# Gated attention and a token-mixing MLP on one core: the order of loads, casts and first pairs in the opening

## The chip, the core and the metric

The kernel runs on one core of one Trainium2 chip. The core has a matrix engine (TensorE, PE in the profile), a vector engine (VectorE, DVE), a scalar engine (ScalarE, ACT), a general engine (GpSimd, POOL) and SyncE (SP), which here only issues DMAs. ACT and POOL issue DMAs too; a DMA that changes the type (v and z from fp32 to fp16) is issued by POOL here. The metric is the device time of one execution in microseconds (us); less is better. Three runs of the kernel before gave a median of 792.01 us.

## The reference

```python
# u, v: (8, 3200, 256), z: (8, 3200, 64)
scores = (1.0 / S) * np.matmul(z, z.transpose(0, 2, 1))
attn = np.maximum(scores, 0.0) ** 2
x = u * np.matmul(attn, v)
# w_q, w_k: (256, 64), w_out: (256, 256)
wq = x @ w_q
wk = x @ w_k
W_tok = (1 / 8) * np.einsum('bsd,btd->bst', wq, wk)
mixed = np.einsum('bst,btd->bsd', W_tok, x)
return np.maximum(mixed, 0.0) @ w_out
```

There is no softmax, so the scores of a batch are a symmetric matrix, and squared ReLU keeps it so.

## The kernel before

**Tiles and groups.** A batch has 3200 rows, which is 25 tiles of 128. The output rows are worked on in seven groups, six of 512 rows and one of 128. For a group, each of the 25 row tiles gives a block of scores, 128 by 512. Scores are made two blocks at a time, called a pair (`use_pair`, L585): two matmuls on the two halves of the array (`scores`, L223) into one of two PSUM buffers (`sc`). The first stage (`first_stage`) takes the pair out of PSUM with ReLU, on ACT (L242) or DVE (L246), into `g`. The second stage (`second_stage`) squares it into fp16, on ACT (L259) or POOL (L261), into one of 14 buffers `at`. The second product (`second_product`, L302) multiplies these blocks with v, into four PSUM banks `acc`. A row tile of a group costs 8 second products, two for each of four 128-column parts.

**Symmetry.** A block of a near group isn't computed twice: SyncE turns it with a transposing DMA (`tt`, `ttl`, L281) and the later group uses the turned block. So a buffer of `at` comes free only when its turned copy has been taken and its second products have run.

**A group's end.** When the second products of half a group are complete, ACT copies one bank out (`both`, L318), DVE adds the other (L319), and POOL multiplies with u (L323) into `x_sb`. SyncE turns x (L348); projections with `wqk` (L365), the products of keys and x (L402), and, a batch later, the mixing (L430) and the output projection with `wo` (L453) follow.

**The order is written by a planner in the kernel.** All engines run their instructions in the order in which the Python code emits them. A loop at the end keeps an estimated clock for each of PE, DVE, ACT and POOL, for SyncE's queue (`sp_at`) and for the DMA engines (`dma_at`), and chooses what to emit next: a pair, a step of second products, or other work. `at_time(t, fn)` emits something when the planner's clock of PE has reached t; `move(ready, due, issue, takes, fn, landed, may)` puts a DMA of SyncE in line, to be emitted after `ready`, in order of `due`. None of these times exists on the chip: there, an instruction waits for its operands and for what stands ahead of it in its engine's queue.

**The opening.** `load_first_z` loads z of batch 0 in four chunks (tiles 0 to 3, 12 to 17, 18 to 24, 4 to 11), one of them from ACT's queue, into buffers with the tag `x_sb`. `load_first_v` loads v from POOL's queue, first tiles 0 and 1, then 2 and 3, and later 12 to 17, 18 to 24 and 4 to 11. `cast_first` (L119) makes two fp16 copies of each z chunk, on DVE, ACT and POOL; `turn_first` turns them on TensorE with an identity (L125) and copies the result into `zT` (L132). Then come the first two pairs. `load_u` (L163) loads u for a group from SyncE's queue into one of two buffers `u_sb`. `load_weights` (L183) loads `wo`, the four parts of `wqk` and the two of `wk2`; the `wo` buffer has the tag `x_sb`. `cast_weights` (L188, L189) casts them on POOL at planner time 38. `batch_begun` plans the next batch's z (load, two copies on DVE, five turned pieces, L155) and its v (five loads from POOL's queue, L138). `open_rows` chooses the row tiles whose second products come next; in the first group of batch 0 it also asks for the planned arrival `v_at` of v. `cold` makes matmuls dearer in the planner's first 11 us.

Of the kernel before, what the change touches and what calls it, by code (L numbers as in the profile page):

```python
# [16 lines left out]
def kernel(  # L17
# [36 lines left out]
    NEARBY = 8  # L54

# [116 lines left out]
    wo32 = {}  # L172

    def load_weights():
        wo32[0] = px.tile([P, ND, D], FP32, tag="x_sb", name="wo32")
        loads = [(wo32[0][:], moe_w_out.rearrange("(c p) e -> p c e", p=P))]
        for r in range(2):
            for w32, w in ((wq32, moe_w_q), (wk32, moe_w_k)):
                loads.append((w32[top(r), :, :], w.rearrange("(c p) h -> p c h", p=dh)))
        for half in range(2):  # L180
            loads.append((wk2[:, :, half, :], moe_w_k.rearrange("(c p) h -> p c h", p=P)))
        for i, (t, w) in enumerate(loads):
            move(18.0 + i, 26.0 + i, 0.65, 0.5, lambda t=t, w=w: nc.sync.dma_start(out=t, in_=w))  # L183

    def cast_weights():
        for r in range(2):
            for w32, half in ((wq32, r), (wk32, 1 - r)):
                nc.gpsimd.tensor_copy(out=wqk[top(r), :, half, :], in_=w32[top(r), :, :])  # L188
        nc.gpsimd.tensor_copy(out=wo[:], in_=wo32[0][:])  # L189
# [334 lines left out]
    keys_at, out_of, turned_at, z_at = {}, {}, {}, {}  # L524
# [49 lines left out]
    def cold():  # L574
        return 2.0 if clock[PE] < 11.0 else 1.0
# [131 lines left out]

    def batch_begun(b, t):
        if b + 1 < B:
            t += 6 if b == 0 else 0  # L710
            at_time(t + 6, lambda: (load_z(b + 1), push(3.0)))
            for half in range(2):
                at_time(
                    t + 18 + 3 * half,
                    lambda half=half: (double_z(b + 1, half), give(DVE, clock[PE], 0.98)),
                )
# [41 lines left out]
    def open_rows():  # L758
# [8 lines left out]
        if b == 0 and gi == 0:  # L767
            ready = [t for t in ready if v_at[t] <= clock[PE]]
# [4 lines left out]
        if len(take) < want:  # L773
            if closing and len(left) - len(take) < 4:
                take = take[: len(left) - 4]
            if not take or (fresh and len(take) < (6 if b or gi else 2)):
                return False
            if not closing:
                take = take[: max(0, len(left) - 4)]
# [61 lines left out]
    load_first_v(0, 2)  # L841
    cast_first(0)
    cast_first(1)
    load_first_v(2, 2)
# [5 lines left out]
    clock[:] = [4.5, 4.95, 4.7, 7.8]  # L850
    v_at = [4.5] * 2 + [8.2] * 2 + [18.7] * 8 + [11.2] * 6 + [14.7] * 7
# [13 lines left out]
    at_time(38.0, cast_weights)  # L865
# [6 lines left out]
    while groups or work or current["left"]:  # L872
# [16 lines left out]
        able = p < NPAIR and z_at[p_chunk(p)] <= now and (p < NAT or all_used(p - NAT) and turned_at.get(p - NAT, 0.0) <= now and not out_of.get(p - NAT))  # L889
# [131 lines left out]
```

## Time and profile before

| | |
|---|---|
| runs | 788.74, 792.01, 792.71 us; median 792.01 |
| the profiled execution | 790.19 us |
| its span, first to last instruction | 787.4 us |
| mean granted clock of TensorE | 0.995 |
| busy, share of the span | PE 97%, DVE 61%, ACT 71%, POOL 80% |
| DMA over the span | 141.52 MB, mean 180 GB/s |

The page gives busy times by engine, the span in 40 slices, the DMA queues, the chain of work that ended last, the costliest groups of instructions by line, and the DMA issues. Other views of the same trace give the instructions in order of time (a timeline, with neighbours of one kind merged), the busy time of each engine in chosen windows, and who waited for whom. PE busy counts a matmul from its start to its modelled end; matmuls overlap, so the count of matmuls in a window says more than its busy time. "SPq" is SyncE's queue: how long the issue of a DMA held it. The granted clock is the share of full speed at which TensorE's clock was let through.

### The profile page before, as it was taken

The numbers are of one execution on the slowest core, as the hardware profiler recorded it, in microseconds if no ns is written. First come the engines' busy times: TensorE is split into PE (matmuls) and PEld (weight loads), VectorE is DVE, ScalarE is ACT, GpSimd is POOL, SyncE is SP. The second block draws the span as 40 slices with busy tenths as digits, with TensorE's granted clock in tenths as the row PEclk, the third lists the DMA queues.
The fourth block names the chain that finished last, engine by engine and source line by source line (L and its number), as shares of the span: only waits on it lengthen the run. The fifth ranks groups of instructions, "written<-read, shape, count | busy, mean of one in ns | idle before, by whom it ended". The sixth has DMA issues, their size and how long they took to land.

```text
span 787.4 us, 28277 instructions
## 1 busy us (share of the span) xinstructions
PE 766.3 (97%) x12373; PEld 659.4 (84%) x12373; DVE 480.9 (61%) x494; ACT 562.9 (71%) x668; POOL 631.0 (80%) x524
## 2 busy tenths in 40 slices
PE   6989999999999999999999999999999999999985
PEld 5879989888898878988899788987889888898883
DVE  5654768566676576755466567656557555675522
ACT  6766677766787757886678667787687876777725
POOL 8878597897889798988689987978789977688640
PEclk9999999999999999999999999999999999999998
DMA  7999999998999999999999998999989999779335
GB/s 196 149 165 165 173 191 162 204 233 167 160 172 224 186 195 178 165 207 187 198 161 182 196 215 176 175 149 222 222 172 155 204 198 198 150 145 199 113 82 196
DMA packets 310075, 141.52 MB, mean 180 GB/s; under 512 B 287808, under 2 KB 290752, under 8 KB 309952
## 3 DMA queue, kind: packets, MB, share of 16 engines
q1 hardware_dynamic: 303040, 123.55, 83.3%
q0 software_dynamic: 6768, 15.98, 13.8%
q8 instruction: 96, 1.57, 0.9%
q14 instruction: 27, 0.22, 0.1%
q10 hardware_dynamic: 144, 0.20, 0.1%
HBM read 59.64 MB, written 26.21 MB: 109 GB/s over the span
## 4 chain that ended last, share of the span: by engine, by line
PE 88%; POOL 3%; DMA 2%; issue 2%; ACT 1%; DVE 1%; SPq 1%; DVEq 0%; POOLq 0%; ACTq 0%
PE acc L302 64%; PE sc L223 12%; PE fo L453 6%; PE qk L365 3%; PE qk L402 2%; POOL at L261 2%; PE mx L430 1%; DVE g L246 1%; DMA v_sb<-in_v_dram 1%; SPq L281 1%; DMA out_dram<-fo 1%; DMA kx<-qk 1%; POOL x_sb L323 0%; DMA z<-in_z_dram 0%; ACT g L242 0%
## 5 line engine op out<-in xcount | busy, mean ns | idle before, releaser
L261 POOL TENSOR_TENSOR at<-g 128x1024 f16<-128x1024 f32 (+2 forms) x240 | 441.1, 1851 | 68.2 <-DVE g L246 58.0
L302 PE MATMUL acc<-v_sb,at 64*128 64x256 f16 x7312 | 492.5, 269 | 2.8 <-DMA v_sb<-in_v_dram 1.9
L246 DVE TENSOR_SCALAR g<-sc 128x1024 f32<-128x1024 f32 (+1 forms) x303 | 357.9, 1197 | 155.7 <-PE sc L223 148.3
L302 PEld LDWEIGHTS <-at 64*128 64x128 f16 x7312 | 394.4, 94 | 60.6 <-issue 7.9
L259 ACT ACTIVATE at<-g 128x1024 f16<-128x1024 f32 (+1 forms) x228 | 234.5, 1035 | 18.9 <-DVE g L246 16.2
L242 ACT ACTIVATE g<-sc 128x1024 f32<-128x1024 f32 (+2 forms) x165 | 165.0, 1002 | 50.6 <-PE sc L223 48.3
L223 PE MATMUL sc<-zT 64*128 64x512 f16 x920 | 178.2, 378 | 2.6 <-DVE g L246 2.1
L323 POOL TENSOR_TENSOR x_sb<-both,u_sb 128x512 f16<-128x512 f32 (+1 forms) x112 | 132.8, 1192 | 50.9 <-DVE both L319 50.6
L302 PE MATMUL acc<-v_sb,tt 64*128 64x256 f16 x2304 | 161.2, 269 | 0.0
L302 PEld LDWEIGHTS <-tt 64*128 64x128 f16 x2304 | 126.7, 94 | 13.0
L319 DVE TENSOR_TENSOR both<-acc,both 128x512 f32<-128x512 f32 (+1 forms) x104 | 69.7, 670 | 86.9 <-ACT both L318 80.8
L318 ACT COPY both<-acc 128x512 f32<-128x512 f32 (+1 forms) x104 | 58.8, 566 | 75.8 <-PE acc L302 73.2
L478 ACT ACTIVATE fo<-fo 128x1024 f32<-128x1024 f32 (+2 forms) x54 | 48.0, 889 | 26.3 <-PE fo L453 23.8
L223 PEld LDWEIGHTS <-zT 64*128 64x128 f16 x920 | 56.5, 94 | 12.2 <-issue 7.9
L443 ACT ACTIVATE rt<-mx 128x1024 f16<-128x1024 f32 (+1 forms) x56 | 52.1, 934 | 8.6 <-PE mx L430 8.0
L453 PE MATMUL fo<-wo,rt 128*128 128x256 f16 x400 | 52.8, 274 | 1.8 <-ACT rt L443 1.8
L378 ACT CAST qk<-qk 128x512 f16<-128x512 f32 (+1 forms) x54 | 29.3, 543 | 34.7 <-PE qk L402 27.3
L453 PEld LDWEIGHTS <-rt 128*128 128x128 f16 x400 | 35.0, 98 | 15.9 <-issue 10.0
L417 DVE TENSOR_TENSOR ha<-qk,ha 128x512 f32<-128x512 f32 x37 | 25.6, 691 | 26.9 <-ACT qk L378 26.0
L365 PE MATMUL qk<-xT_sb,wqk 64*128 64x256 f16 (+1 forms) x404 | 32.0, 265 | 0.5 <-DMA xT_sb<-x_sb 0.5
L395 POOL COPY kx<-kx 128x128 f16<-128x128 f16 (+1 forms) x101 | 26.1, 285 | 7.3 <-DMA kx<-qk 7.3
L402 PE MATMUL qk<-x_sb,kx 64*128 64x256 f16 x360 | 29.0, 269 | 0.0
(43 smaller groups left out, 218.4 us busy)
## 6 DMA issues: line engine op xcount, KB each, us to landing
u_sb<-in_u_dram SPq DMA_DIRECT2D x48, 512.0 KB, 4.7
out_dram<-fo SPq DMA_DIRECT2D x40, 512.0 KB, 5.2
v_sb<-in_v_dram POOLq DMA_DIRECT2D x35, 320.0 KB, 6.1
out_dram<-fo SPq DMA_DIRECT2D x16, 256.0 KB, 2.0
zn<-in_z_dram POOLq DMA_DIRECT2D x7, 400.0 KB, 6.1
tt<-at SPq DMA_TRANSPOSE x144, 4.5
u_sb<-in_u_dram SPq DMA_DIRECT2D x8, 128.0 KB, 3.7
out_dram<-fo SPq DMA_DIRECT2D x8, 128.0 KB, 1.9
```

The costliest lines, as they stand in the source:

```text
L223: nc.tensor.matmul(out=sc[:, h, 0:gw], lhsT=zT[b][top(h), ts(ti, P)], rhs=zT[b][top(h), ds(gs, gw)], start=True, stop=True,)
L242: nc.scalar.activation(out=g[:, hs, 0:w], in_=sc[:, hs, 0:w], func=RELU, scale=GSCALE)
L246: nc.vector.tensor_scalar(out=g[:, hs, 0:w], in0=sc[:, hs, 0:w], scalar1=0.0, scalar2=GSCALE, op0=AOP.max, op1=AOP.mult,)
L259: nc.scalar.square(out=out, in_=g[:, hs, 0:w])
L261: nc.gpsimd.tensor_mul(out=out, in0=g[:, hs, 0:w], in1=g[:, hs, 0:w])
L302: nc.tensor.matmul(out=accs[half, r][:, ds((j % 2) * D, D)], lhsT=weights(b, gi, ti, j)[top(r), :], rhs=vs[b][top(r), ti, :], start=(first ...
L318: nc.scalar.copy(out=both[:, 0 : n * D], in_=accs[half, 0][:, 0 : n * D])
L319: nc.vector.tensor_add(out=both[:, 0 : n * D], in0=accs[half, 1][:, 0 : n * D], in1=both[:, 0 : n * D])
L323: nc.gpsimd.tensor_mul(out=xs[b, gi][:, 0:n, :, r, :].rearrange("p n c d -> p (n c) d"), in0=both[:, 0 : n * D].rearrange("p (m d) -> p m ...
L365: nc.tensor.matmul(out=ps[:, r, 0 : n * P], lhsT=wqk[top(r), c, :, :].rearrange("p t h -> p (t h)"), rhs=xTs[b, gi][top(r), 0:n, c, :], st ...
L443: nc.scalar.activation(out=out, in_=ps[:, 0:nr, 0 : ND * n * P], func=RELU)
L453: nc.tensor.matmul(out=banks[r][:, ds(j * D, D)], lhsT=flat[:, ds((dc * n + j) * P, P)], rhs=wo[:, dc, :], start=(dc == 0 and j == 0), sto ...
```

## The change

- **v of batch 0.** Tiles 0 to 3 come in one load instead of two; the other three loads keep their order on POOL's queue.
- **z and u of batch 0.** The third and fourth chunk of z are loaded into buffers with the tag `u_sb`, so that the first two loads of u reuse them.
- **TensorE.** 28 matmuls of the identity with itself stand ahead of everything else.
- **First pairs.** `first_stage` can split a pair's two blocks between ACT and DVE. `use_pair` does so up to planner time 24 where by its clocks the two halves end sooner than the whole. In the emitted order DVE has eight more instructions of its kind, 128 by 512.
- **Weights.** `wo` gets a buffer with the tag `fo`, is loaded at 76 to 80 and cast on POOL at 90. The two halves of `wk2` are loaded at 110 to 130. The cast of `wqk` is at 40 instead of 38.
- **z and v of batch 1.** z is loaded at 24, as before, and its five turned pieces are planned 4 us apart instead of 6. Its five v loads are planned 8 us apart from 64 instead of 13 us apart from 38. For later batches these times stay.
- **The planner's knowledge.** `v_at` now holds the planned arrival of v for every batch, and the first group of each batch asks for it. `z_here` holds back the pairs of a batch until the last turned piece of its z has landed by the planner's clock. `cold` is 1.4 for 9 us instead of 2.0 for 11, and the planned arrivals of the first v are other numbers. `KEEP` names the number 4.

```diff
     def load_first_z():
         for i, (n0, nn) in enumerate(ZCH):
-            z32[n0] = px.tile([P, nn, dqk], FP32, tag="x_sb", name="z32")
+            pool, tag = (px, "x_sb") if i < 2 else (pu, "u_sb")
+            z32[n0] = pool.tile([P, nn, dqk], FP32, tag=tag, name="z32")
...
     def load_weights():
-        wo32[0] = px.tile([P, ND, D], FP32, tag="x_sb", name="wo32")
-        loads = [(wo32[0][:], moe_w_out.rearrange("(c p) e -> p c e", p=P))]
+        loads = []
         for r in range(2):
             for w32, w in ((wq32, moe_w_q), (wk32, moe_w_k)):
                 loads.append((w32[top(r), :, :], w.rearrange("(c p) h -> p c h", p=dh)))
+        for i, (t, w) in enumerate(loads):
+            move(18.0 + i, 26.0 + i, 0.65, 0.4, lambda t=t, w=w: nc.sync.dma_start(out=t, in_=w))
         for half in range(2):
-            loads.append((wk2[:, :, half, :], moe_w_k.rearrange("(c p) h -> p c h", p=P)))
-        for i, (t, w) in enumerate(loads):
-            move(18.0 + i, 26.0 + i, 0.65, 0.5, lambda t=t, w=w: nc.sync.dma_start(out=t, in_=w))
+            t, w = wk2[:, :, half, :], moe_w_k.rearrange("(c p) h -> p c h", p=P)
+            move(110.0, 130.0, 0.65, 0.4, lambda t=t, w=w: nc.sync.dma_start(out=t, in_=w))
+        wo32 = pg.tile([P, 2, W], FP32, tag="fo", name="wo32", bufs=2)[:, 0, :]
+        wo32 = wo32.rearrange("p (c e) -> p c e", c=ND)
+        w = moe_w_out.rearrange("(c p) e -> p c e", p=P)
+        move(76.0, 80.0, 0.65, 0.8, lambda: nc.sync.dma_start(out=wo32, in_=w))
+        at_time(40.0, cast_weights)
+        at_time(90.0, lambda: (nc.gpsimd.tensor_copy(out=wo[:], in_=wo32), give(POOL, 0.0, 0.6)))
...
-    def first_stage(p, sc, on_act):
+    def first_stage(p, sc, ways):
         g = pg.tile([P, 2, W], FP32, tag="g", name="g")
-        for hs, w in pieces(p):
+        parts = pieces(p)
+        if len(ways) > len(parts):
+            parts = [(slice(h, h + 1), parts[0][1]) for h in range(2)]
+        for (hs, w), on_act in zip(parts, ways * 2):
...
-        on_act = choose(*(max(clock[x], ready) for x in (ACT, DVE)))
-        done = give(ACT, ready, 1.03) if on_act else give(DVE, ready, 1.2)
-        g = first_stage(p, sc, on_act)
+        a, d = (max(clock[x], ready) for x in (ACT, DVE))
+        if clock[PE] < UNTIL and max(a + 0.57, d + 0.68) + SPLIT < min(a + 1.03, d + 1.2):
+            ways = [a < d, a >= d]
+            done = max(give(ACT, ready, 0.57), give(DVE, ready, 0.68))
+        else:
+            ways = [choose(a, d)]
+            done = give(ACT, ready, 1.03) if ways[0] else give(DVE, ready, 1.2)
+        g = first_stage(p, sc, ways)
...
+    Z0 = 24
+    V0 = 64
+    V1 = 8
+
     def batch_begun(b, t):
         if b + 1 < B:
-            t += 6 if b == 0 else 0
-            at_time(t + 6, lambda: (load_z(b + 1), push(3.0)))
+            t0 = max(t + 6, Z0)
+            at_time(t0, lambda: (load_z(b + 1), push(3.0)))
...
+            step = 6 if b else 4
             for i in range(5):
-                move(t + 24 + 6 * i, t + 40 + 6 * i, 1.28, 1.05, lambda i=i: turn_z(b + 1, i))
+                move(
+                    t0 + 18 + step * i, t0 + 34 + step * i, 1.28, 1.05,
+                    lambda i=i: turn_z(b + 1, i),
+                    lambda t, i=i: z_ready.update({(b + 1, i): t}),
+                )
             for i in range(5):
-                at_time(t + 20 + 13 * i, lambda i=i: (load_v(b + 1, 5 * i, 5), push(2.5)))
+                at = t + 20 + 13 * i if b else V0 + V1 * i
+                at_time(at, lambda i=i: v_loaded(b + 1, 5 * i, 5))
...
+    def z_here(p):
+        b = tiles[2 * p + 1][0]
+        return not b or z_ready.get((b, 4), 1e9) <= clock[PE]
...
     make_identity(nc, ident)
     load_first_z()
-    load_first_v(0, 2)
+    load_first_v(0, 4)
+    warm = acc_tile(0, 0, "warm")
+    for _ in range(28):
+        nc.tensor.matmul(out=warm[:, 0:P], lhsT=ident[:], rhs=ident[:], start=True, stop=True)
     cast_first(0)
     cast_first(1)
-    load_first_v(2, 2)
     cast_first(2)
```

More of the change, by code (lines that the diff above doesn't have):

```diff
@@ L54 @@
     NEARBY = 8
+    KEEP = 4
     consts = ctx.enter_context(tc.tile_pool(name="consts", bufs=1))
@@ L188, in cast_weights @@
                 nc.gpsimd.tensor_copy(out=wqk[top(r), :, half, :], in_=w32[top(r), :, :])
-        nc.gpsimd.tensor_copy(out=wo[:], in_=wo32[0][:])
+        give(POOL, 0.0, 1.4)
     def is_turned(gi, gj):
@@ L574, in cold @@
     def cold():
-        return 2.0 if clock[PE] < 11.0 else 1.0
+        return 1.4 if clock[PE] < 9.0 else 1.0
+    SPLIT = 0.0
+    UNTIL = 24.0
     def choose(a, d):
@@ L766, in open_rows @@
         ready = [t for t in left if row_at.get((b, gi, t), 1e9) <= clock[PE]]
-        if b == 0 and gi == 0:
-            ready = [t for t in ready if v_at[t] <= clock[PE]]
+        if gi == 0:
+            ready = [t for t in ready if v_at.get((b, t), 1e9) <= clock[PE]]
         mine = [t for t in ready if (b, gi, t) in made]
@@ L778, in open_rows @@
             if not closing:
-                take = take[: max(0, len(left) - 4)]
+                take = take[: max(0, len(left) - KEEP)]
         for t in take:
@@ L849 @@
     load_first_v(4, 8)
-    clock[:] = [4.5, 4.95, 4.7, 7.8]
-    v_at = [4.5] * 2 + [8.2] * 2 + [18.7] * 8 + [11.2] * 6 + [14.7] * 7
+    clock[:] = [4.5, 4.95, 4.7, 7.2]
+    for t, n0, nn in ((6.5, 0, 4), (18.0, 4, 8), (10.5, 12, 6), (14.0, 18, 7)):
+        v_at.update({(0, n): t for n in range(n0, n0 + nn)})
     dma_at[0] = 16.0
```

18 lines of the change are left out of this document (11 added, 7 removed).

## The prediction

> **What bounds the kernel now.** The first part of the page, busy time by engine, comes first:
>
> ```profile
> PE 766.3 (97%) x12373; PEld 659.4 (84%) x12373; DVE 480.9 (61%) x494; ACT 562.9 (71%) x668; POOL 631.0 (80%) x524
> ```
>
> TensorE is the bound: of a span of 787.4 us it is idle for 21. A change of the opening can win only what TensorE loses there, as idle time or at half clock. The list of who waited for whom, for TensorE in the first 60 us (total, times, longest), has nearly all the idle time ahead of the drain at the end:
>
> ```profile
> PE ztp L125 <- ACT zd L119: 4.2, 1, 4.2
> PE sc L223 <- DVE g L246: 2.1, 3, 1.1
> PE acc L302 <- DMA v_sb<-in_v_dram: 1.9, 1, 1.9
> PE acc L302 <- DVE both L319: 0.8, 2, 0.5
> ```
>
> From 100 to 700 us the windows table has TensorE idle for 0.23 us in all. So there are three places: the wait for v near 10 us, a group's end near 25 us, and a wait for the first stage near 50 us. The timeline of the opening (start, duration, engine, line) shows the first:
>
> ```profile
> 1.44 0.72 POOL L107 DMA_DIRECT2D v_sb<-in_v_dram  x1
> 2.15 0.91 SPq L163 DMA_DIRECT2D u_sb<-in_u_dram  x2
> 4.36 0.53 POOL L107 DMA_DIRECT2D v_sb<-in_v_dram  x1
> 5.39 1.04 PE L223 MATMUL sc<-zT 64*128 64x512 f16 x4
> 7.56 1.92 POOL L261 TENSOR_TENSOR at<-g 128x1024 f16<-128x1024 f32 x1
> 8.07 0.62 PE L223 MATMUL sc<-zT 64*128 64x512 f16 x4
> 10.58 0.61 PE L302 MATMUL acc<-v_sb,at 64*128 64x256 f16 x8 [1.89 <-DMA v_sb<-in_v_dram]
> ```
>
> Two small v loads surround 1 MB of u. The chain of waits puts 6.09 us, from 4.36 to 10.45, on the second; `at` of the first pair was ready at 9.48. The same four score matmuls take 1.04 us at 5.39 and 0.62 at 8.07: TensorE starts at half clock. The windows table (window, length, busy and count of PE, PEld, DVE, ACT, POOL, then clock, DMA share, GB/s) shows the other two:
>
> ```profile
> 24.00:27.40 3.40, 2.68 (x40) 1.91 (x36) 2.07 (x3) 3.37 (x6) 3.38 (x4) 1.00 0.61 135
> 27.40:38.00 10.60, 10.60 (x190) 10.07 (x187) 6.05 (x6) 6.70 (x8) 9.98 (x11) 1.00 1.04 138
> 48.30:52.50 4.20, 2.47 (x34) 1.64 (x30) 2.50 (x3) 3.33 (x4) 2.22 (x2) 1.00 1.17 108
> 52.50:56.00 3.50, 3.09 (x26) 1.65 (x22) 2.73 (x3) 1.74 (x2) 3.50 (x3) 0.51 1.04 177
> ```
>
> The costliest is 48.3 to 56: the idle gaps are followed by a stretch with a granted clock of 0.51. From 48.39 to 57.01 TensorE runs 16 score and 50 second-product matmuls; at the steady pitches (a pair of scores 0.22 us, 22 second products 1.20 us, both from the chain of waits) that is 4.5 us of work in 8.6: 4.1 us lost. Why there is no better work shows on SyncE's queue:
>
> ```profile
> 33.56 1.96 SPq L183 DMA_DIRECT2D wk<-in_moe_w_k_dram  x2
> 36.91 0.59 POOL L138 DMA_DIRECT2D v_sb<-in_v_dram  x1
> 38.76 6.27 SPq L281 DMA_TRANSPOSE tt<-at  x2
> 46.43 0.59 POOL L138 DMA_DIRECT2D v_sb<-in_v_dram  x1
> 46.44 6.41 SPq L281 DMA_TRANSPOSE tt<-at  x2
> 63.46 2.60 SPq L281 DMA_TRANSPOSE tt<-at  x2
> ```
>
> SyncE issues without a pause from 18 to 67 us, and two transposes that meet a v load hold it for 6.3 and 6.4 us where two alone take 2.6. The 14 buffers of `at` stay occupied, no scores are made between 43.2 and 48.3, and then eight pairs stand with little second product between them: DVE and ACT can't clear the two score buffers that fast.
>
> **The change part by part.** All against the profiled execution: span 787.4, its time 790.19.
>
> *First v as one load, u later: +1.4.* One DMA issue (0.53) leaves POOL's queue ahead of the first square, which can start at about 7.0 instead of 7.56. Splitting the first pairs brings their g forward (DVE half 0.67 and ACT half 0.57, the means of the 512-wide DVE and ACT rows, beside one of 1.23; ACT is busy with zT until 6.30), to 6.9 instead of 7.27. The square ends at 7.0+1.9=8.9 and TensorE starts at about 9.1, not 10.58: 1.5, less 0.1 for a later zT. The v for it is issued at 1.44 as before; with the 7.2 us that the 384 KB load took it lands at 8.6, in time. Ends: 0 (v still last) and 2.0 (ACT's square at 8.58 decides).
>
> *u behind z: −0.4.* u's tiles now reuse buffers of z chunks 2 and 3, so SyncE holds until their casts end (about 5.0 and 6.1 instead of 2.15); behind it stand only one small load and the first transpose at 18. u's reader runs at 26.75, far later. But 1 MB of u now meets the v load of tiles 12 to 17, issued at about 4.9. By that load's own 7.2 us it lands at 12.1; TensorE wants it after 32 second products (1.75) and five pairs (1.1), at 11.9. Between 0 (it lands sooner) and −1.5 (delayed as the 128 KB load was, by 6 us for a third of the bytes) I take −0.4, the nearer row.
>
> The Trainium skill (DMA: Bandwidth & Descriptors, Queues, rings and completion order) says that each engine goes round-robin over its queues; by that u would not hold v up, this term would be 0 and the result 786.1. The 6.09 us for 128 KB speak against an even share here.
>
> *Warming: 0.* 28 matmuls at 0.107 us (ten transposes took 1.30 with their tail) last from 1.4 to 4.4, beside TensorE's wait for z until 4.16. The excess of 0.25 is covered by DVE, whose cast until 4.92 holds the copy of zT anyway; uncovered it would cost 0.25. If the clock rises sooner, the second transposes and two pairs save up to 0.8, but POOL's square then decides. Ends: +0.6, and −1.0 if the clock falls again in the gap before 9.1 (as at 52.5, 3.4 us at half speed, partly idle).
>
> The Trainium skill (TensorE: Matmul & The Clock Gate, Why this matters for your kernels) lets the clock fall only behind gaps of some 3 us; by that the end of −1.0 would be gone and the sum would stay. The trace disagrees: the clock of 0.51 stands behind gaps of TensorE of at most 1.10 us.
>
> *Split pairs later on: +0.2.* Eight pairs are split. Each costs 1.25 of engine time instead of 1.03 to 1.23 and is done some 0.5 sooner. ACT and DVE have 3.0 and 3.9 us free of 13.4 between 10.6 and 24, which hides the cost. Ends −0.5 and +0.6.
>
> *Group end at 25: +0.3.* 40 matmuls stand in 3.4 us where the pitch of the next window (18 per us) would give 61, some of it scores: about 1.1 lost. The two copies out of PSUM (0.59+0.69 each) remain; two more pairs now stand ready. Ends 0 and 1.1.
>
> *SyncE's queue from 33 to 53: +3.3.* The wk2 loads leave (1.96), v of batch 1 goes from here to 64 us and later (6.27+6.41−2×2.60=7.5), together 9 us of a queue that was 20 us long. In the instruction order of the changed kernel the bunch of eight pairs is gone: the densest place left has seven pairs and a projection in 4.6 us of TensorE work, against 0.55 us per pair from ACT and DVE together (1.03 and 1.23). I take 0.8 of the 4.1 as remaining. Ends 0 (the stall only moves) and 4.1.
>
> *Later: −0.4.* Five v loads stand 8 us apart from 64 us, where three were. Two more transposes are held by about 3.6 each, while z's own five (1.3 each) stand one to five places earlier in SyncE's order, which takes one or two of them out of this stretch. The `wo` load (0.5 on SyncE) and cast (0.61 on POOL) come in at 76 and 90; POOL is busy 22.24 of 30 there. Ends 0 and −3.7 (a stall like that at 50, less 0.4).
>
> *After 100 us* the same instructions are dealt anew: 0, ends ±1.5. The drain is in the same order.
>
> Sum: 1.4−0.4+0+0.2+0.3+3.3−0.4=+4.4: 785.8 for the profiled execution. That one lies 1.8 below the median of the three runs (792.01); 4.4 off the median is 787.6. The four executions' mean is 790.9 and would give 786.5, which I predict.
>
> **The rivals.**
>
> *The stall moves to 64 to 100 us.* For it: SyncE issues almost without pause there too (60.8 to 92.5), and each v load stretches a transpose. Against it: TensorE lost nothing from 64 to 94 with three such loads. It takes the 3.3 back: 786.5+3.3=789.8.
>
> *u only changes places with v.* The wait for v is replaced by one for tiles 12 to 17: −1.5 instead of −0.4 and 0.3 off the first term, 1.4 in all: 787.9. For it the 6.09 us; against it the first v load, which now has no u in front.
>
> *Batch 1 waits for its v: slower.* Its first second products stood at 102.0 and come at about 97.6. The last v load is placed at 96, on POOL's queue behind squares of 1.87. In the profile these loads ran 1 to 5 us ahead of their places and landed in 6.1 us (median), at 102 then. Tiles 20 to 24 are wanted 20×0.44 plus some ten pairs at 0.22 after 97.6, at 108.6: 6.6 spare. It decides if POOL runs 5 us late and the load takes the 11.5 us of the slowest: 112.5, 3.9 idle and 1.7 at half clock; if group 1 then starves likewise, as its rows need the same tiles, twice that, 11: 786.5+5.6 to +11, 792 to 797.
>
> **How the numbers follow.** Forecast 0.60; moved stall 0.19; v behind u 0.12; batch 1 late 0.05; anything else in the new order 0.04. A measurement can tell 0.5%, 4.0 us, so faster means below 788.05. The forecast's own range is 783 to 789.5 and is 0.82 of the time beyond the bound (0.49); v behind u half of the time (0.06); the moved stall in a sixth (0.03): faster 0.58. Slower by 0.5% (above 796): half of batch 1 late and of the rest, and the worst of the moved stall, 0.06. Within: 0.36. The range for 8 in 10 is 782 to 791: below, 4 us for the best ends of the first and sixth terms and the spread of the runs; above, the moved stall.
>
> **What would show it.** Right: the first `acc` near 9.1, no TensorE wait for g near 50 and no clock of 0.5 there, pairs of transposes near 2.6 us between 33 and 53, and batch 1 starting 4 us sooner. Wrong: a wait of `acc` for v near 12, transposes of 4 to 5 us after 64 followed by a gap, a clock at half between 5 and 12, or a gain by 100 us that is lost later.

## The result, and the profile after

| | before | after |
|---|---|---|
| median of 7 runs each, side by side | 792.35 us (788.74 to 796.42) | 797.14 us (794.88 to 799.40) |
| the profiled execution, its span | 790.19, 787.4 us | 797.81, 796.0 us |
| mean granted clock | 0.995 | 0.986 |

The ratio is 1.0056, 95% interval 1.0030 to 1.0081: slower by about half a per cent, where a gain of 4.4 us was forecast. A second set of runs of the kernel after gave 795.93 us and 1.0054 [1.0029, 1.0079].

To place the loss, each pair of scores gets a *lag*: the time at which its first matmul starts, less the TensorE work that the emitted order puts ahead of it at the steady pitches (0.107 us for a score matmul, 0.053 for a second product and so on; warming not counted). The lag grows where TensorE idles or runs at half clock, and slowly where one kind of product follows another: from pair 80 to pair 453 of before TensorE is idle for 0.14 us at a granted clock of 1.00, and yet the lag grows by 24.3 us over some 1000 such changes (10.3 of them over 313 changes from second products to scores). All work at these pitches is 729.4 us. From single profiled executions, in us:

| stretch | before | before, again | after | after, again | forecast |
|---|---|---|---|---|---|
| lag at pair 27 (about 41 us) | 10.9 | 12.6 | 13.5 | 12.9 | 1.5 won |
| pair 27 to 40 (to about 62 us) | +4.7 | +4.6 | +2.1 | +2.1 | 3.3 won |
| pair 40 to 80 (to about 124 us) | +2.3 | +1.4 | +5.9 | +5.1 | 0.4 lost |
| pair 80 to 453 (to about 739 us) | +24.3 | +24.2 | +25.1 | +26.9 | 0 |
| the end: span, less 729.4, less the lag at pair 453 | 15.7 | 15.7 | 20.0 | 19.4 | 0 |
| span | 787.4 | 788.0 | 796.0 | 795.9 | 783.0 |

So the stall near 50 us did shrink, by 2.5 us. The stretch around 80 us and the end lost, and the opening lost 2.6 us against the first profile of before, 0.3 to 0.9 against the second. Of the 13.0 us between the forecast span and the measured one, about 4.1 lie in the opening, 0.7 in the stretch to pair 40, 3.2 in that to pair 80, 0.8 in the long middle and 4.3 at the end.

The windows table (columns as before: window, length, busy and count of PE, PEld, DVE, ACT, POOL, clock, DMA share, GB/s), first before:

```profile
8.00:20.00 12.00, 10.11 (x160) 8.56 (x160) 8.47 (x8) 9.20 (x10) 10.61 (x6) 1.00 0.81 171
20.00:60.00 40.00, 36.69 (x573) 31.71 (x570) 23.95 (x24) 27.62 (x32) 33.50 (x27) 0.96 1.10 156
60.00:100.00 40.00, 39.55 (x675) 37.66 (x671) 24.24 (x27) 26.99 (x32) 28.22 (x26) 1.00 1.13 166
```

and after:

```profile
8.00:20.00 12.00, 10.41 (x110) 6.94 (x112) 8.42 (x12) 9.19 (x12) 10.48 (x8) 0.72 0.78 170
20.00:60.00 40.00, 38.65 (x629) 34.28 (x626) 27.71 (x29) 28.54 (x34) 31.02 (x23) 1.00 0.97 162
60.00:100.00 40.00, 37.17 (x608) 34.90 (x604) 18.67 (x18) 27.68 (x34) 34.76 (x28) 0.96 0.99 159
```

The counts tell what busy time hides: from 8 to 20 us TensorE does 110 matmuls instead of 160, at a mean clock of 0.72. From 20 to 60 it does 56 more, from 60 to 100 it does 67 fewer, and the clock of 0.96 has moved from the one window to the other.

TensorE's waits after (total, times, longest), for 0 to 60 us, 60 to 100 and 754 to the end:

```profile
PE ztp L127 <- POOL zd L121: 2.1, 1, 2.1
...
PE sc L230 <- DVE ha L425: 2.8, 1, 2.8
...
PE fo L463 <- ACT rt L453: 3.3, 3, 2.4
PE hd L412 <- POOL kx L405: 1.9, 1, 1.9
```

The wait for v near 10 us is gone, and so is the wait for the first stage near 50. New against this profile of before are the waits for GpSimd's `zd` (the second profile of before has one of 1.44 us too), for `ha` and for `kx`; the one of `fo` for `rt` cost 1.8 before.

**The opening.** The timeline after:

```profile
4.66 0.54 POOL L109 DMA_DIRECT2D v_sb<-in_v_dram  x1
4.83 4.44 SPq L165 DMA_DIRECT2D u_sb<-in_u_dram  x2
8.01 0.43 DVE L121 CAST zd<-z 128x512 f16<-128x512 f32 x1 [2.59 <-DMA z<-in_z_dram]
8.04 0.87 POOL L121 CAST zd<-z 128x512 f16<-128x512 f32 x1 [2.85 <-DMA z<-in_z_dram]
8.36 1.28 DVE L256 TENSOR_SCALAR g<-sc 128x512 f32<-128x512 f32 x2
8.97 0.62 PE L127 MATMUL ztp<-ident,zd 128*128 128x128 f16 x8 [2.10 <-POOL zd L121]
9.92 1.91 POOL L271 TENSOR_TENSOR at<-g 128x1024 f16<-128x1024 f32 x1
11.42 0.82 PE L312 MATMUL acc<-v_sb,at 64*128 64x256 f16 x6 [0.48 <-ACT at L269]
```

z's last chunk (tiles 4 to 11) lands late, and both engines that cast it take their work in order: VectorE's `g` of the first pair and GpSimd's first square stand behind the casts. The first second product comes at 11.42, not at the forecast 9.1, and waits for `at`, not for v. What the wait of 2.10 us does to the clock is in the windows table after:

```profile
6.10:9.40 3.30, 1.20 (x19) 0.83 (x15) 1.39 (x3) 0.66 (x2) 1.35 (x3) 1.00 0.94 238
9.50:16.20 6.70, 6.08 (x46) 3.35 (x46) 3.88 (x6) 5.28 (x9) 5.89 (x4) 0.50 1.01 226
```

Warming raised the clock near 6.1 us (seven transposes at 6.31 take 0.56 us; without warming, in e2_no_warm below, 0.93). Behind the gap it fell again for 6.7 us, over the first second products. The Trainium skill (TensorE: Matmul & The Clock Gate, Why this matters for your kernels) warns of gaps over some 3 us; here the clock fell behind 3.30 us in which TensorE was busy for 1.20 and no gap was longer than 2.10.

**Near 80 us,** the timeline after:

```profile
67.41 3.65 SPq L291 DMA_TRANSPOSE tt<-at  x2
71.16 2.96 SPq L393 DMA_TRANSPOSE kx<-qk  x1
74.20 4.84 SPq L291 DMA_TRANSPOSE tt<-at  x1
79.07 1.06 ACT L269 ACTIVATE at<-g 128x1024 f16<-128x1024 f32 x1 [3.54 <-DMA tt<-at]
80.63 0.69 DVE L425 COPY ha<-qk 128x512 f32<-128x512 f32 x1 [5.18 <-ACT qk L388]
81.38 1.04 PE L230 MATMUL sc<-zT 64*128 64x512 f16 x4 [2.83 <-DVE ha L425]
```

ScalarE's square at 79.07 waits for a buffer of `at`, which comes free when its turned copy has landed: that of the block issued at 67.41, which took 11.6 us. Behind it in ScalarE's order stands the copy `qk`, behind that VectorE's `ha`, and for `ha` TensorE waits. From 81.2 to 84.5 the granted clock is 0.50.

**The end.** The timeline after:

```profile
754.06 13.92 SPq L358 DMA_TRANSPOSE xT_sb<-x_sb  x3
768.03 1.26 SPq L393 DMA_TRANSPOSE kx<-qk  x1
770.58 0.53 POOL L405 COPY kx<-kx 128x128 f16<-128x128 f16 x2 [3.13 <-DMA kx<-qk]
770.93 0.63 PE L412 MATMUL hd<-x_sb,kx 64*128 64x256 f16 x8 [1.95 <-POOL kx L405]
786.02 1.86 PE L463 MATMUL fo<-wo,rt 128*128 128x256 f16 x8 [2.43 <-ACT rt L453]
```

and before, where the last turned keys stand ahead of the last turned x:

```profile
748.49 12.59 SPq L348 DMA_TRANSPOSE xT_sb<-x_sb  x2
761.17 1.62 SPq L383 DMA_TRANSPOSE kx<-qk  x1
762.88 1.22 SPq L348 DMA_TRANSPOSE xT_sb<-x_sb  x1
```

In the new order the keys come last on SyncE's queue, and TensorE waits 1.95 us for them.

### The profile page after: what moved, and what is told of

It reads as the page before. It is cut to its first block, busy times and chain, and to the rows that moved or that the text cites. A ratio compares the mean times of both kernels' runs of the same rounds, so it can differ in the third digit from the quotient of the medians.

```text
span 796.0 us, 28358 instructions
## 1 busy us (share of the span) xinstructions
PE 774.4 (97%) x12401; PEld 667.5 (84%) x12401; DVE 490.3 (62%) x504; ACT 561.0 (70%) x670; POOL 624.6 (78%) x519
## 3 DMA queue, kind: packets, MB, share of 16 engines
q1 hardware_dynamic: 303040, 123.55, 81.2%
## 4 chain that ended last, share of the span: by engine, by line
PE 92%; DMA 3%; ACT 2%; DVE 1%; issue 1%; POOL 1%; SPq 0%; ACTq 0%; POOLq 0%; DVEq 0%
PE acc L312 67%; PE sc L230 13%; PE fo L463 6%; PE qk L375 3%; PE qk L412 2%; DMA tt<-at 1%; PE mx L440 1%; DMA z<-in_z_dram 1%; POOL at L271 1%; ACT rt L453 1%; DMA out_dram<-fo 1%; DVE g L256 0%; ACT g L252 0%; DMA kx<-qk 0%; DVE both L329 0%
## 5 line engine op out<-in xcount | busy, mean ns | idle before, releaser
L312 PE MATMUL acc<-v_sb,at 64*128 64x256 f16 x7312 | 499.3, 270 | 1.5 <-DVE both L329 0.9
L271 POOL TENSOR_TENSOR at<-g 128x1024 f16<-128x1024 f32 (+2 forms) x236 | 435.0, 1854 | 74.5 <-DVE g L256 55.3
L256 DVE TENSOR_SCALAR g<-sc 128x1024 f32<-128x1024 f32 (+2 forms) x313 | 367.4, 1189 | 140.0 <-PE sc L230 128.6
L312 PEld LDWEIGHTS <-at 64*128 64x128 f16 x7312 | 399.7, 94 | 58.9 <-issue 10.1
L269 ACT ACTIVATE at<-g 128x1024 f16<-128x1024 f32 (+1 forms) x232 | 237.8, 1036 | 22.7 <-DVE g L256 16.0
L252 ACT ACTIVATE g<-sc 128x1024 f32<-128x1024 f32 (+2 forms) x163 | 158.4, 975 | 53.8 <-PE sc L230 49.2
L230 PE MATMUL sc<-zT 64*128 64x512 f16 x920 | 182.9, 380 | 3.5 <-DVE ha L425 2.8
L230 PEld LDWEIGHTS <-zT 64*128 64x128 f16 x920 | 59.4, 94 | 13.5 <-issue 8.6
L463 PE MATMUL fo<-wo,rt 128*128 128x256 f16 x400 | 54.4, 280 | 3.3 <-ACT rt L453 3.3
```

What stands on the lines that cost most here:

```text
L230: nc.tensor.matmul(out=sc[:, h, 0:gw], lhsT=zT[b][top(h), ts(ti, P)], rhs=zT[b][top(h), ds(gs, gw)], start=True, stop=True,)
L252: nc.scalar.activation(out=g[:, hs, 0:w], in_=sc[:, hs, 0:w], func=RELU, scale=GSCALE)
L256: nc.vector.tensor_scalar(out=g[:, hs, 0:w], in0=sc[:, hs, 0:w], scalar1=0.0, scalar2=GSCALE, op0=AOP.max, op1=AOP.mult,)
L269: nc.scalar.square(out=out, in_=g[:, hs, 0:w])
L271: nc.gpsimd.tensor_mul(out=out, in0=g[:, hs, 0:w], in1=g[:, hs, 0:w])
L312: nc.tensor.matmul(out=accs[half, r][:, ds((j % 2) * D, D)], lhsT=weights(b, gi, ti, j)[top(r), :], rhs=vs[b][top(r), ti, :], start=(first ...
```

## The experiments

Times are medians of 9 to 12 executions, ratios are against the kernel before in the same set of runs. Each of these kernels was profiled in one execution only; those of e2_no_warm, e5_two_v_no_warm, e6_z_late, m2_cast_behind and n1_one_v_warm were the slowest of theirs, so lags and waits from them needn't be typical. Where an edit changes a DMA's place or leaves out the warming, the order of all other instructions stays as in the kernel it starts from, except in m2_cast_behind. In the experiments' texts "theory A" is: one 512 KB load of v (as read, in fp32; the prediction counts what is written in fp16, half as much) delays z's last chunk, and warming costs as well.

**e1_two_v: the first v in two loads (kernel after otherwise).**

```diff
-    load_first_v(0, 4)
+    load_first_v(0, 2)
...
     cast_first(1)
+    load_first_v(2, 2)
```

> The changed kernel with its first v load (tiles 0 to 3) put back into two loads at their old places on POOL's queue; every other engine's order stays. Theory A: the one load of 512 KB of v runs beside z's last chunk and delays it (its DVE cast stood at 8.01 us instead of 5.40), and as that cast stands ahead of the first stage on DVE and ahead of two v loads on POOL, everything in the opening is late and TensorE falls back to half clock. Then the cast comes back to about 5.4, the first g to about 6, the first second product to 9.5 to 10.6, and 2 to 4 us of the time are won. Rival B: z's last chunk is late because of where its buffer is or because u's reissue collides with it; then the cast stays near 8 and the time within 1 us.

791.02 us, 1.0000 [0.9978, 1.0021]. VectorE's cast of z's last chunk stands at 6.49 us instead of 8.01, not back at 5.4; the first second product comes at 9.89. The opening has no stretch of granted half clock, the lag at pair 27 is 11.2, and from pair 40 to 80 only 1.8 us are lost, though no instruction there has changed its place.

**e2_no_warm: no warming (kernel after otherwise).** The tile `warm` and its 28 matmuls are left out.

> The changed kernel without the 28 matmuls of the identity. Theory A (z's late last chunk makes the gap, and the clock falls in any case): the score matmuls near 5.5 run at half clock as before (1.04 us for four), the second products still begin near 11.4, the time changes by less than 1 us. Rival C (warming is what hurts: it shifts the clock's rise so early that it falls again in the gap from 6.9 to 9): without it the clock rises once, near 8 to 12 us, and stays, and 2 to 3 us are won.

792.09 us, 1.0020 [0.9991, 1.0049]. The cast stands at 6.60, though the one load is still there, and the lag at pair 27 is 11.3. The first ten second products, at 10.00, take 0.72 us where they take 1.25 in the kernel after. So the opening was better, as rival C has it, but its clock and its earlier chunk came together here; and the ratio lies 0.0034 below that of the kernel after, inside the intervals.

**e3_v1_early: batch 1's v loads back at 38 us and every 13 (kernel after otherwise).**

```diff
+                if not b:
+                    at_time(38 + 13 * i, lambda i=i: load_v(1, 5 * i, 5))
...
     def v_loaded(b, n0, nn):
-        load_v(b, n0, nn)
+        if b > 1:
+            load_v(b, n0, nn)
```

> The changed kernel with batch 1's five v loads put at planner times 38, 51, 64, 77 and 90, as before the change; only their places in POOL's queue differ, the order on every other engine stays. Theory D (a v load beside a turned block holds the block, SyncE's queue and the buffer of at): the wait of TensorE near 79 to 85 us (4.5 us lost there, behind a turned block that took 11.6 us to land) shrinks to 1 us or less, and slow transposes and a loss of 1 to 4 us come back between 38 and 60 us; in all 0 to 3 us are won. Rival E (the order of the instructions makes the bunch, wherever the v loads are): 3 us or more are still lost between 76 and 86 us.

794.32 us, 1.0039 [1.0013, 1.0065]. SyncE's queue in its timeline:

```profile
49.80 4.80 SPq L291 DMA_TRANSPOSE tt<-at  x2
```

The same two transposes take 2.62 at 49.65 in the kernel after. They were held again, yet the stall didn't come back: pair 27 to 40 lost 2.1 us, as in the kernel after. From 40 to 80 it lost 2.7 instead of 5.9.

**e4_keys_first: the last turned keys ahead of the last turned x (kernel after otherwise).** In the loop of the drain the turned keys count as due 4 us sooner.

```diff
-            x = min(later + ripe, key=lambda x: x[0])
+            x = min(later + ripe, key=lambda x: x[0] - (4.0 if len(x) > 4 and x[4] in key_fns else 0.0))
```

> The changed kernel with the last turned keys issued ahead of the last turned x in the drain, the order that stood before the change; nothing else moves. Theory F: the drain is 4.2 us longer in the changed kernel's profile because the planner put the keys behind an x that POOL finishes only at 766.7 us; TensorE's wait of 1.95 us for the doubled keys goes, and 1.5 to 2.5 us are won. Rival G: stores and the clock set the drain's length, and what is won at 770 us is waited for again at 783 us: 0 to 0.5 us.

794.03 us, 1.0019 [0.9994, 1.0045]. The wait of `hd` is gone, the end costs 17.8 instead of 20.0; the wait of `fo` for `rt` stays (2.0). The ratio lies 0.0037 below that of the kernel after in its first set of runs, inside the intervals.

**a2_after_again: the kernel after again.**

> The changed kernel as it is, for pairing with the others and to see what of its profile repeats. If z's last chunk is late by what is loaded beside it, its cast on DVE stands near 8 us again and the first second product near 11.4; if that was one unlucky execution, near 5.4 and 9.5. The drain's wait for keys (1.95 us) is there again, the wait behind ACT's square near 79 us too, at some size.

795.93 us, 1.0054 [1.0029, 1.0079]. The cast stands at 7.47, the clock is half from 8.95 to 15.78, 5.1 us are lost between pairs 40 and 80, and the waits for `ha` (1.9) and `kx` (1.9) are there. The losses are the kernel's, not one execution's.

**e5_two_v_no_warm: two v loads and no warming together.**

> The changed kernel with the first v in two loads and without the 28 warming matmuls. In the first experiments z's last packet came at 4.9 us with two loads and no warming (the kernel before), 6.0 with two loads and warming, 6.1 with one load and no warming, 7.3 to 7.5 with both. If both delay z, each by 1.2 us (theory H), it comes at 4.9 here, DVE's cast at 5.4, the first g at 6, and the opening is 1 to 2 us better than with two loads alone. If u's place behind z counts too (rival I), it stays at 5.5 to 6.5.

790.61 us, 0.9973 [0.9957, 0.9989]. The cast stands at 6.56: later than theory H expected (5.4). The opening alone turns a loss into a gain, but not through the chunk as priced.

**e6_z_late: batch 1's five turned pieces of z at the planner's 74 to 82 (kernel after otherwise).**

```diff
-                    lambda i=i: turn_z(b + 1, i),
+                    lambda i=i: b and turn_z(b + 1, i),
...
+                if not b:
+                    at_time(74 + 2 * i, lambda i=i: turn_z(1, i))
```

> The changed kernel with the five turned pieces of batch 1's z put from planner times 42 to 58 to 74 to 82, behind the turned blocks of SyncE's queue; nothing else moves. Theory J: these three pieces ahead of the blocks (1.3 us each) make the block late for which ACT's square waits near 79 us (3.5 us, then TensorE 2.8 us and half a clock window); then that block is issued some 4 us sooner, ACT's wait falls below 0.5 us, and 2 to 4 us are won in the stretch from 74 to 86. Rival D: the v loads beside the blocks make it; then ACT still waits for 2 us or more. If batch 1's scores wait for z instead, TensorE shows a wait for zT near 86 us.

792.63 us, 1.0004 [0.9977, 1.0031]. The waits for `ha` and for the buffer of `at` are gone, and pair 40 to 80 loses 1.3 us. SyncE's queue in its timeline:

```profile
63.74 4.29 SPq L291 DMA_TRANSPOSE tt<-at  x2
...
69.44 1.26 SPq L291 DMA_TRANSPOSE tt<-at  x1
70.79 3.88 SPq L157 DMA_TRANSPOSE zT<-zd  x2
```

In the kernel after, three pieces of z stood ahead of these blocks, at 53.67, 58.21 and 60.89. The block for which ScalarE waited there went out at 67.41, beside a v load issued at 67.82, and landed 11.6 us later; here it goes out at 63.74, ahead of the v load at 67.98, and lands after 5.5. So z's pieces made it late; how much the v load beside it added isn't separated.

**b1_v1_late: the kernel before with batch 1's v loads at 64 us and every 8.** This is the larger part of the forecast's largest step (7.5 of 9 us of SyncE's queue), made alone; the loads of `wk2` stay.

```diff
-                at_time(t + 20 + 13 * i, lambda i=i: (load_v(b + 1, 5 * i, 5), push(2.5)))
+                at_time(t + 20 + 13 * i, lambda i=i: (b and load_v(b + 1, 5 * i, 5), push(2.5)))
+                if not b:
+                    at_time(64 + 8 * i, lambda i=i: load_v(1, 5 * i, 5))
```

> The kernel before, with batch 1's five v loads at planner times 64 to 96 as the change has them; only POOL's queue differs. Theory D (as in the prediction: two v loads at 37 and 46 us stretch the turned blocks on SyncE's queue, and that makes the stall): the blocks take 1.3 to 2 us each, and of the 4.1 us lost from 48.4 to 57 at most 1.5 stay. Rival E (the planner's order, with eight pairs in a bunch, makes it): 3 us or more are still lost between 46 and 58.

792.06 us, 0.9996 [0.9975, 1.0018]. The queue ran free, as forecast, and the stall stayed; its timeline:

```profile
44.23 2.61 SPq L281 DMA_TRANSPOSE tt<-at  x2
...
50.02 1.71 SPq L281 DMA_TRANSPOSE tt<-at  x1
51.83 1.22 SPq L281 DMA_TRANSPOSE ttl<-at  x1
53.14 1.26 SPq L281 DMA_TRANSPOSE tt<-at  x1
53.93 0.39 PE L223 MATMUL sc<-zT 64*128 64x512 f16 x2 [1.10 <-DVE g L246]
```

Two transposes take 2.61 where they took 6.27 and 6.41, no scores stand between 44.70 and 50.37 all the same, and then come eight pairs that wait for their first stage. Pair 27 to 40 loses 4.6 us, as in the kernel before. TensorE had second products and a projection to do all through that time: no scores stand there in its emitted order. So the stall is in the emitted order, not in the v loads or in a queue that is held.

**m1_all_four: all four repairs together.** Two v loads, no warming, z's pieces late, keys first; the rest of the change stays.

> The kernel after with four of its parts undone or mended together: the first v load is again two loads at their old places, no warming products, batch 1's five turned pieces of z at the planner's 74 to 82, and in the drain the last turned keys ahead of the last turned x. All else of the change stays. Theory A (one v load and warming cost the opening, the z pieces cost 78 to 82 us, the key order costs the drain, and these are separate): 0.9973 (two loads, no warming) less some 4 us of lost time between pair 40 and pair 80 (5.9 and 5.1 in two profiles of the kernel after, 1.3 with the z pieces late) and up to 1.9 us of the wait for the keys in the drain, of which earlier single edits returned about half each at the end: ratio 0.991 to 0.995, 785 to 788 us. Rival (the later stages take back what a stage before them wins, since the drift from 124 us on and the drain follow the planner and not the opening): 0.996 to 0.999, 789 to 791 us, with the lag at pair 80 near 13 us all the same.

787.36 us, 0.9944 [0.9921, 0.9967], span 785.6: faster than both kernels. The lag at pair 27 is 10.6; pair 27 to 40 loses 2.1, pair 40 to 80 1.3, the end costs 15.9. The list of TensorE's waits between 60 and 100 us is empty. The single gains against the kernel after are 0.0081 (e5_two_v_no_warm) and 0.0050 (e6_z_late), in one set of runs with it, and 0.0037 (e4_keys_first, against its first set); added, they would give 1.0054−0.0168, 0.989. They seem to overlap, though the intervals, some 0.005 each way for the sum, hardly show it: with the better opening of e1_two_v and e5_two_v_no_warm the stall near 80 us was already smaller (1.8 and 3.4).

**m2_cast_behind: as m1_all_four, with the casts of z's last chunk moved behind the first pairs.**

```diff
-    cast_first(3, [0])
     load_first_v(18, 7)
     load_first_v(4, 8)
+    cast_first(3, [0])
...
     turn_first(0)
-    cast_first(3, [1])
...
     turn_first(2)
+    use_pair()
+    cast_first(3, [1])
...
+    use_pair()
     turn_first(3)
```

> As m1_all_four, and the casts of z's last chunk (tiles 4 to 11) moved behind: GpSimd issues the two v loads first, VectorE casts its half behind the first stage of three pairs, and TensorE turns the chunk behind four pairs of scores. Theory (the late cast holds the first pairs, since VectorE and GpSimd take their work in order): the first stage of pair 0 no longer waits for the chunk, the first second product starts 0.5 to 1.5 us before that of m1_all_four, and the lag at pair 8 is 0.5 to 1.5 us smaller; ratio 0.001 to 0.002 below m1_all_four. Rival (the half clock and the first squares bound the opening, not the cast): lag at pair 8 within 0.3 us of m1_all_four, and the new order further on decides the ratio, either way by up to 0.003.

790.99 us, 0.9991 [0.9970, 1.0011]: slower than m1_all_four. The first second product comes at 13.49 instead of 9.13, and the lag at pair 8 is 12.0 instead of 8.9. VectorE's cast met two squares on GpSimd; its timeline:

```profile
7.51 3.76 POOL L271 TENSOR_TENSOR at<-g 128x1024 f16<-128x1024 f32 x2
9.28 2.30 DVE L121 CAST zd<-z 128x512 f16<-128x512 f32 x1
11.72 1.01 PE L127 MATMUL ztp<-ident,zd 128*128 128x128 f16 x8 [3.50 <-DVE zd L121]
```

The wait only moved behind it and grew. Whether an early first stage is worth anything by itself this run doesn't tell.

**b2_one_v: the kernel before with tiles 0 to 3 of v in one load.** `load_first_v(0, 2)` becomes `load_first_v(0, 4)`, `load_first_v(2, 2)` goes.

> The kernel before with tiles 0 to 3 of v in one load at the place of the first, everything else and the order on every engine as before. Theory A (the one 512 KB load ahead of z's last chunk delays that chunk by some 1.2 us and the first pairs with it): z's last chunk lands near 6 us or later, ratio 1.001 to 1.003. Rival I (when that chunk lands varies from execution to execution by itself, and the load has no part in it): ratio 0.999 to 1.001. Rival G (the forecast's own step: an issue on GpSimd saved and the first second products 0.5 us earlier): 0.998 to 0.9995.

790.88 us, 0.9975 [0.9949, 1.0002]; the cast at 7.74. The chunk is late, but there is no loss, so theory A's price doesn't hold for the kernel before.

**b0_before_again: the kernel before again, profiled a second time.**

> The kernel before again, one look: in its one profile z's last chunk landed at 4.9 us, in that of b1_v1_late, with the same opening, at 7.8. Theory A (the landing is set by the loads ahead of it): near 5 again, lag at pair 8 near 8.4 us, with a stall of about 4 us between pairs 26 and 40. Rival I (it varies by itself): anywhere from 5 to 8 us.

One execution, 790.97 us, the cast at 7.98, lag at pair 27 12.6. The kernel before shows that cast at 5.40, 7.98 and, with the same opening, 8.25 (b1_v1_late): the one profile from which the forecast was made was a lucky opening.

**Four kernels that put one or two parts back into m1_all_four,** in one set of runs (m1_all_four's own row in the table is from the set before). For u, in n2_u_early, z's chunks get buffers of the x pool again:

```diff
-            pool, tag = (px, "x_sb") if i < 2 else (pu, "u_sb")
-            z32[n0] = pool.tile([P, nn, dqk], FP32, tag=tag, name="z32")
+            z32[n0] = px.tile([P, nn, dqk], FP32, tag="x_sb", name="z32")
```

n1_one_v_warm:

> m1_all_four with its opening put back as in the kernel after: the first v one load, 28 warming products. The later repairs (z pieces late, turned keys first) stay. Theory K (the two parts together make z's last chunk land at 7.0 to 7.5 us instead of 5.3 to 6.2, and the pairs behind it start later): chunk lands at 7 or later, lag at pair 8 near 11 us against 8.9, the end 1.5 to 3 us later than m1_all_four, ratio 0.9965 to 0.9985. Rival (what the opening loses the later stages take back): ratio 0.9935 to 0.996.

n2_u_early:

> m1_all_four with the one thing that holds u back taken away: z's chunks 2 and 3 lie in buffers of the x pool again, so u's two loads are issued right behind z's, as in the kernel before. Theory U (u's 1 MB behind z takes shares of the engines' time from z's last chunk and the first v): the chunk lands at 7.2 to 7.8 us as in three of four profiles of that opening, lag at pair 8 near 10 us, ratio 0.996 to 0.998. Rival (u's place costs nothing): chunk near 6 us or earlier, lag at pair 8 near 9 us, ratio 0.9935 to 0.9955.

n3_warm:

> m1_all_four with the 28 warming products alone put back. Theory K (it needs both parts): z's last chunk at 5.3 to 6.2 us; the first products at the full clock save 0.5 to 0.8 us; ratio 0.9935 to 0.9955. Rival W (the products alone delay the chunk or drop the clock again): chunk at 7 us or a half clock between 9 and 13 us, lag at pair 8 above 10 us, ratio 0.996 to 0.998.

n4_one_v:

> m1_all_four with the first v as one load alone. Theory K (it needs both parts): z's last chunk at 5.3 to 6.2 us, lag at pair 8 8.9 to 9.6 us, ratio 0.994 to 0.9955. Rival V (one load of 512 KB alone delays the chunk): chunk at 7 us or later, lag at pair 8 above 10 us, ratio 0.996 to 0.998. The forecast's own step (one issue on GpSimd saved, 0.5 us): 0.993 to 0.994.

| kernel | u | first v | warming | cast of the chunk | lag at pair 8 | median, ratio |
|---|---|---|---|---|---|---|
| m1_all_four | late | two loads | no | 5.73 | 8.9 | 787.36, 0.9944 [0.9921, 0.9967] |
| n3_warm | late | two loads | yes | 6.52 | 9.5 | 788.74, 0.9958 [0.9939, 0.9978] |
| n4_one_v | late | one load | no | 8.22 | 11.6 | 788.80, 0.9953 [0.9932, 0.9973] |
| n1_one_v_warm | late | one load | yes | 7.92 | 11.3 | 790.19, 0.9981 [0.9962, 0.9999] |
| n2_u_early | early | two loads | no | 7.31 | 11.6 | 788.47, 0.9960 [0.9943, 0.9978] |

The cast in the timelines of n3_warm and of n4_one_v:

```profile
6.52 0.43 DVE L121 CAST zd<-z 128x512 f16<-128x512 f32 x1 [1.02 <-DMA z<-in_z_dram]
```

```profile
8.22 0.43 DVE L121 CAST zd<-z 128x512 f16<-128x512 f32 x1 [2.92 <-DMA z<-in_z_dram]
```

Theory K (it needs both parts) falls as to the chunk: one load alone puts it late, warming alone doesn't. Over all profiles that keep the cast's place, with u late the cast stands at 5.7 to 6.6 in four of four with two loads, and at 7.5 to 8.2 in seven of eight with one (6.60 in e2_no_warm is the exception); with u early it stands at 7.3 to 8.3 in four of five (5.40 in the first profile of before is the exception). So either of u and the one load, ahead of the chunk's landing, is mostly enough. With u late the chunk and the first load of v land together: at 5.71 and 5.88 in m1_all_four, at 8.20 and 8.41 in n4_one_v. In time the single parts can't be told from each other or surely from m1_all_four (0.9953 to 0.9960, intervals of 0.002 each way); both together end 1.4 us behind the next, with intervals that still touch. Taken with the earlier runs there are four pairs of kernels, all with u late, that differ in the one load alone, and it is the slower way in all four: by 0.0054 and 0.0047 of the time with z's pieces early (a2_after_again against e1_two_v, e2_no_warm against e5_two_v_no_warm; the intervals don't touch), by 0.0023 and 0.0009 with them late (n1_one_v_warm against n3_warm, n4_one_v against m1_all_four; inside the intervals). How large a part of the loss the opening is in the median stays open to that degree.

## Why the prediction was wrong

Four steps failed: the opening's loads, priced by the issue that they save; the stretch behind 64 us, priced at −0.4; the drain, put at nothing; and the cause, though hardly the size, of the +3.3.

*First v as one load, u later, +1.4: wrong in sign.* The step counted GpSimd's saved issue (0.53) and took for given that z's chunk lands as in the profile of before, at 5.4. The transfer that was enlarged runs beside that chunk, and what waits for the chunk stands on three engines in order. In place of a gain, the one load cost 3.7 to 4.3 us of the median in the kernel after and its like (0.0047 and 0.0054); with u early it cost nothing (b2_one_v). By the profiles it is u's move that helps, and the one load takes that away: with u late and two loads the cast came at 5.7 to 6.6, and m1_all_four has its first second product at 9.13, where the step wanted it. With z's pieces late the one load costs 2.7 us of lag at pair 8 in the profile (n4_one_v against m1_all_four); part of it is TensorE's pace (eight second products take 0.60 at 10.46 in m1_all_four, ten 1.25 at 11.62 in n4_one_v). The medians show 1.4, which is inside their intervals.

*u behind z, −0.4.* Not seen: no second product waited for the v of tiles 12 to 17 in the kernel after.

*Warming, 0.* The end that the forecast named for it came true: the clock fell again in the gap before the first second product. Without a late chunk it doesn't: eight second products take 0.61 us at 11.04 in n3_warm, 1.06 at 12.88 in the kernel after. But no run showed a gain from warming either: in all four pairs of kernels that differ by it alone the one with warming is slower, by 0.0014 to 0.0034, each time inside the intervals. Why stays open.

*Split pairs and the group's end, +0.5 together.* Between pair 8 and pair 27 the lag grew by 1.7 us instead of 2.5: +0.8, right in kind; no run tries the two parts by themselves.

*SyncE's queue from 33 to 53, +3.3: size nearly right, cause wrong.* 2.5 us were won, but not by the v loads that left. With them away and the old order, the stall is whole (b1_v1_late); with them back and the new order, it is gone (e3_v1_early). The forecast had seen both, the free queue and the missing bunch of eight pairs, and credited the first. Which part of the change rid the order of the bunch isn't separated.

*Later, −0.4 with an end of −3.7: mis-sized.* It measured some −3.5 (−3.7 between the second profiles), by the rival that the stall moves to 64 to 100 us. The v loads there were the suspects. With two of the five back at 44 and 54 us the loss fell to 2.7, which says little, since it fell to 1.8 in e1_two_v and to 4.1 in e4_keys_first, where nothing there had moved. With z's own pieces out of the way it was 1.3 in e6_z_late, m1_all_four and the four kernels made from that, and both waits vanished. "One to five places earlier in SyncE's order" was booked as a relief of this stretch, and it is what puts the turned blocks back.

*"The drain is in the same order": wrong.* The last keys and the last x had changed places on SyncE's queue. Of the 4.3 us lost at the end, the keys explain 2 to 3: it costs 17.8 in e4_keys_first, and 17.3 to 21.6 (mean 19.6) in the seven profiles of the new order with the keys last, 15.8 to 18.2 (mean 16.8) in the seven with the keys first, m2_cast_behind among them. Why `fo` waits longer for `rt`, behind stores, was seen but not tested by itself.

*Against the median.* The forecast was made against one execution. Its opening was 1.7 us better than that of the second profile, so part of the gain that it promised on top wasn't there to be had.

## What to carry to other kernels

A transfer that is made larger or sooner is priced by what runs beside it and by everything queued behind the work that waits for it, not by the issue it saves. Where a planner deals the work anew, compare the emitted order of each queue through to the last instruction, and test a claimed cause both ways: take it out of the old order, put it back into the new. A landing time read from one profile is one draw; look at it in a second execution before a step is built on it.

## What the hardware showed beyond this

- The same program's load of 256 KB landed so that its cast stood at 5.40 or at 7.98 us.
- In m2_cast_behind VectorE's cast of 128x512 to fp16 took 2.30 us beside GpSimd's squares, where it takes 0.43. It ended at 11.58, 0.3 us behind GpSimd's second square (7.51 + 3.76 = 11.27). The Trainium skill (SBUF — State Buffer, Terms) says that the two engines lock a shared pair of ports for a whole instruction and the loser blocks; this run agrees.
- The granted clock reads 1.00 ahead of its first recorded change, whatever the pace: from 11 to 13 us it does so in n4_one_v, where the ten second products at 11.62 take 1.25 us; in n3_warm, at 9.92, ten take 0.72. At the start of a kernel the pace of the matmuls tells more than that column.
- In some executions TensorE waits some 2 us for a store to end (ScalarE's `fo` needs the store before it) or for a turned tile to land, in others of the same order not at all. Between 100 and 740 us n4_one_v has no such wait, and n1_one_v_warm, with the same order there, two:

```profile
PE mx L440 <- ACT fo L488: 2.1, 1, 2.1
PE qk L375 <- DMA xT_sb<-x_sb: 1.8, 1, 1.8
```

This is enough to move a single execution by 4 us, nearly as much as the whole effect that was studied.
